# A new hand-written order for every instruction of a Fourier filter and a gated MLP that share one core

## The chip, the cores and the metric

The kernel runs on one core of a Trainium2 chip. The metric is device time in microseconds (us) of one execution. Three runs of the kernel before took 201.26, 201.38 and 201.50 us, median 201.38. The profiled execution took 201.59 us, of which 199.8 us lie between its first and its last instruction; that stretch is called the span, and times "at 125.7 us" count from its start.

## The reference, cut to what matters

```python
def _A_ref(x, w_r, w_i):                       # x: 1 x 2048 x 640
    X = jnp.fft.rfft2(x.astype(jnp.float32), axes=(-2, -1))
    X = X * (w_r + 1j * w_i)                   # weights: 2048 x 321
    return jnp.fft.irfft2(X, s=(S, D), axes=(-2, -1)).astype(jnp.bfloat16)

def _B_ref(x, w_gate, w_up, w_down):           # 640 x 1536, 640 x 1536, 1536 x 640
    g = jnp.einsum("bsd,df->bsf", x, w_gate)
    u = jnp.einsum("bsd,df->bsf", x, w_up)
    return jnp.einsum("bsf,fd->bsd", g * u, w_down)

xn = _layernorm(A_x)                           # over the 640 columns
return A_x + _A_ref(xn, A_w_r, A_w_i) + _B_ref(xn, B_w_gate, B_w_up, B_w_down)
```

Inputs and output are bfloat16. Both branches take the same normalized rows, and their results are summed with the input.

## The kernel before, in words

**Tasks.** `_build` makes a list of 971 tasks. A task is one copy, one transfer, or a short group of instructions for one engine, and has a number, a name, and the tasks that it depends on. The names used below:

- `T0_b` transposes a normalized block of 128 rows on TensorE, and `eT0_b` copies the result from PSUM to SBUF. There are 16 blocks b.
- `GU_f_r_u` (L945) is one gate or up product (u is 0 or 1) for a slice f of 128 hidden columns and four blocks of rows from r: five matmuls with 512 columns. `eG_f_r_u` copies it out of PSUM, and `H_f_r` (L985) multiplies gate by up on VectorE.
- The Fourier branch: `S1` to `S5` on VectorE and `R_b` (L899) with its copy `eR_b` are the forward transform's first stage. `D_t_w` (L1028) with its copies `eD_t_w_g`, then `C_t` (L1047), finish it. `WM_t` (L1064, L1067; five VectorE instructions that read PSUM) multiplies by the filter weights, and `SM_t` (L1080, L1081) combines the parts. `JA`, `JB`, `JC` and `JD` are four copies that mirror the result, the last two on GpSimd. `IA_q` (L1110) with the copy `eIA_q`, `I_a` (L1138) with the copy `eI_a`, and `V1` to `V5` on VectorE go back.
- `ACC_a_h_k` (L1215) is a part of the down projection for row block a and half h: k is the first of its hidden slices, counted in the order 7 to 11, 0 to 6. `IV_a_h` (L1227) adds the Fourier branch's last step in the same PSUM bank. `FINA_a_h` on ScalarE copies the sum out, `FIN_a` (L1254) on VectorE adds the input block that `ld_xr a` fetched, and `st_out a` writes it. Two output buffers are used in turn, so `FINA_5_0` waits until the store of block 3 has landed.

**Order.** Nothing is scheduled at run time. `_PLAN` is a literal table of 971 triples (task number, engine, PSUM bank), with engine 0 = TensorE (PE), 1 = ScalarE (ACT), 2 = VectorE (DVE), 3 = GpSimd (POOL), 4 = SyncE (SP), and bank -1 where the task takes none. `replay` reads it from top to bottom: each engine's instructions stand in the order in which their triples stand. It also adds the dependences that follow from the banks: a task that takes a bank waits for the copies that empty that bank's last owner. `compute_waits` turns the dependences into semaphore waits. So a triple that moves changes an engine's order, a changed second number moves a copy to another engine, and a changed third number makes a matmul wait for other copies. The cost functions (`_d_act` and the others) are not used at run time.

**Engines.** Copies out of PSUM and two of the mirror copies may stand on ACT or on DVE; L682 is the ACT form, L683 the other. SP issues 131 of the 133 transfers, strictly in its list's order: a transfer that waits for a buffer holds up all that stand behind it.

**Shared memory.** The down-projection weights lie in buffer `WD`. The tables for `IA` lie in the same place, in its first part, so `ld_wd0` waits for `IA_0` to `IA_9`, `ld_wd2` for `IA_10` to `IA_19`, `ld_wd4` for `IA_20` to `IA_29` and `ld_wd6` for `IA_30` and `IA_31`. Only `ld_wd7` (slices 7 to 11) is free of them. The first `ACC_a_h_5` needs `ld_wd0` and `ld_wd2`; the first `ACC_a_h_9` needs `ld_wd4` and `ld_wd6`. The filter weights of two steps t share one of three buffers, so `ld_w14_*` waits for `WM_8` and `WM_9`, and `WM_15` and `WM_14` wait for all `ld_w14_*`.

Of the kernel before, what the change touches and what calls it, by code (L numbers as in the profile page):

```python
# [400 lines left out]
def _d_act(n):  # L401
# [4 lines left out]
    (10, 0, 0), (11, 4, -1), (18, 2, -1), (12, 1, -1), (19, 2, -1), (20, 2, -1), (0, 3, -1), (8, 3, -1), (13, 4, -1),  # L406
    (182, 1, -1), (14, 4, -1), (15, 4, -1), (181, 4, -1), (21, 1, -1), (22, 2, -1), (23, 2, -1), (24, 0, 2), (9, 0, 7),
    (25, 2, -1), (26, 2, -1), (193, 0, 6), (27, 1, -1), (28, 1, -1), (29, 1, -1), (30, 2, -1), (31, 2, -1), (32, 0, 0),
    (43, 1, -1), (44, 1, -1), (183, 4, -1), (36, 2, -1), (34, 2, -1), (33, 2, -1), (35, 2, -1), (45, 1, -1), (46, 2, -1),
    (37, 2, -1), (47, 2, -1), (191, 0, 3), (192, 1, -1), (194, 1, -1), (38, 1, -1), (39, 2, -1), (195, 2, -1), (40, 2, -1),  # L410
    (124, 2, -1), (203, 0, 4), (196, 0, 2), (48, 0, 5), (197, 1, -1), (204, 1, -1), (49, 1, -1), (201, 0, 0), (202, 1, -1),
    (41, 0, 2), (42, 1, -1), (205, 2, -1), (184, 4, -1), (16, 4, -1), (53, 2, -1), (125, 2, -1), (54, 2, -1), (198, 0, 3),
    (199, 1, -1), (200, 2, -1), (64, 1, -1), (55, 2, -1), (50, 2, -1), (51, 2, -1), (208, 0, 1), (209, 1, -1), (206, 0, 7),
    (207, 1, -1), (65, 1, -1), (218, 0, 2), (219, 1, -1), (66, 1, -1), (67, 1, -1), (216, 0, 4), (217, 1, -1), (68, 1, -1),
    (210, 2, -1), (126, 2, -1), (52, 2, -1), (127, 2, -1), (56, 1, -1), (57, 2, -1), (69, 2, -1), (58, 2, -1), (73, 2, -1),
    (70, 2, -1), (128, 2, -1), (211, 0, 3), (212, 1, -1), (213, 0, 0), (214, 1, -1), (215, 2, -1), (186, 4, -1), (223, 0, 5),
    (185, 4, -1), (221, 0, 7), (224, 1, -1), (17, 4, -1), (76, 1, -1), (74, 0, 5), (71, 0, 6), (1, 4, -1), (129, 0, 3),
    (131, 0, 1), (222, 1, -1), (75, 2, -1), (220, 2, -1), (133, 2, -1), (61, 2, -1), (225, 2, -1), (134, 2, -1), (59, 0, 7),
    (72, 1, -1), (77, 1, -1), (132, 1, -1), (130, 1, -1), (78, 1, -1), (60, 2, -1), (135, 2, -1), (226, 0, 5), (227, 1, -1),
    (79, 1, -1), (80, 1, -1), (81, 2, -1), (228, 0, 0), (229, 1, -1), (230, 2, -1), (187, 4, -1), (62, 0, 6), (63, 1, -1),  # L420
    (231, 0, 1), (232, 1, -1), (136, 2, -1), (188, 4, -1), (7, 4, -1), (82, 2, -1), (233, 0, 3), (234, 1, -1), (88, 1, -1),
    (235, 2, -1), (137, 2, -1), (142, 2, -1), (238, 0, 4), (239, 1, -1), (236, 0, 0), (5, 4, -1), (190, 4, -1), (189, 4, -1),
    (241, 0, 1), (237, 1, -1), (89, 1, -1), (240, 2, -1), (85, 2, -1), (138, 0, 2), (139, 1, -1), (243, 0, 5), (244, 1, -1),
    (90, 1, -1), (242, 1, -1), (245, 2, -1), (143, 2, -1), (246, 0, 0), (247, 1, -1), (91, 1, -1), (140, 0, 2), (248, 0, 4),
    (249, 1, -1), (250, 2, -1), (144, 2, -1), (100, 1, -1), (251, 0, 6), (252, 1, -1), (253, 0, 0), (256, 0, 7), (481, 4, -1),
    (258, 0, 4), (92, 1, -1), (101, 1, -1), (141, 1, -1), (254, 1, -1), (257, 1, -1), (102, 1, -1), (255, 2, -1), (145, 2, -1),
    (93, 2, -1), (259, 1, -1), (260, 2, -1), (146, 2, -1), (261, 0, 5), (97, 2, -1), (263, 0, 1), (262, 1, -1), (449, 4, -1),
    (452, 4, -1), (3, 4, -1), (448, 4, -1), (450, 4, -1), (264, 1, -1), (103, 1, -1), (104, 1, -1), (105, 2, -1), (268, 0, 0),
    (269, 1, -1), (265, 2, -1), (106, 2, -1), (94, 2, -1), (155, 2, -1), (273, 0, 3), (151, 0, 4), (274, 1, -1), (152, 1, -1),
    (149, 0, 1), (150, 1, -1), (266, 0, 0), (267, 1, -1), (112, 1, -1), (270, 2, -1), (156, 2, -1), (153, 0, 5), (147, 0, 3),  # L430
    (154, 1, -1), (278, 0, 7), (279, 1, -1), (95, 0, 1), (96, 1, -1), (113, 1, -1), (271, 0, 2), (272, 1, -1), (275, 2, -1),
    (109, 2, -1), (276, 0, 6), (277, 1, -1), (280, 2, -1), (157, 2, -1), (485, 4, -1), (148, 1, -1), (281, 0, 0), (86, 0, 7),
    (114, 1, -1), (282, 1, -1), (283, 0, 2), (284, 1, -1), (115, 1, -1), (116, 1, -1), (285, 2, -1), (117, 2, -1), (158, 2, -1),
    (118, 2, -1), (159, 2, -1), (121, 2, -1), (453, 4, -1), (441, 4, -1), (482, 4, -1), (695, 4, -1), (444, 4, -1), (446, 4, -1),
    (443, 4, -1), (480, 4, -1), (442, 4, -1), (447, 4, -1), (478, 4, -1), (445, 4, -1), (2, 4, -1), (83, 0, 1), (110, 0, 6),
    (98, 0, 5), (291, 0, 3), (292, 1, -1), (84, 1, -1), (87, 1, -1), (111, 1, -1), (288, 0, 0), (289, 1, -1), (286, 0, 2),
    (287, 1, -1), (290, 2, -1), (99, 1, -1), (296, 0, 3), (297, 1, -1), (293, 0, 1), (294, 1, -1), (168, 2, -1), (295, 2, -1),
    (119, 0, 0), (120, 1, -1), (122, 0, 2), (162, 0, 3), (163, 1, -1), (298, 0, 7), (299, 1, -1), (164, 0, 0), (165, 1, -1),
    (166, 0, 5), (167, 1, -1), (303, 0, 4), (107, 0, 0), (300, 2, -1), (169, 2, -1), (451, 4, -1), (454, 4, -1), (304, 1, -1),
    (108, 1, -1), (301, 0, 3), (302, 1, -1), (160, 0, 4), (305, 2, -1), (170, 2, -1), (123, 1, -1), (308, 0, 6), (309, 1, -1),  # L440
    (161, 1, -1), (306, 0, 3), (307, 1, -1), (310, 2, -1), (316, 0, 2), (317, 1, -1), (313, 0, 1), (314, 1, -1), (171, 2, -1),
    (172, 2, -1), (323, 0, 5), (324, 1, -1), (321, 0, 7), (173, 0, 5), (179, 0, 0), (180, 1, -1), (175, 0, 3), (176, 1, -1),
    (322, 2, -1), (311, 0, 2), (174, 2, -1), (177, 0, 0), (509, 4, -1), (513, 4, -1), (4, 4, -1), (484, 4, -1), (312, 2, -1),
    (325, 2, -1), (315, 2, -1), (318, 0, 7), (319, 2, -1), (320, 2, -1), (178, 1, -1), (455, 0, 5), (457, 1, -1), (458, 0, 3),
    (460, 1, -1), (459, 1, -1), (456, 2, -1), (489, 0, 1), (346, 0, 0), (491, 2, -1), (490, 1, -1), (328, 0, 7), (329, 1, -1),
    (347, 1, -1), (461, 0, 4), (462, 2, -1), (333, 0, 3), (334, 1, -1), (463, 0, 6), (486, 0, 1), (487, 1, -1), (488, 1, -1),
    (331, 0, 0), (332, 1, -1), (464, 2, -1), (479, 4, -1), (483, 4, -1), (512, 4, -1), (510, 4, -1), (541, 4, -1), (514, 4, -1),
    (465, 2, -1), (468, 3, -1), (469, 3, -1), (466, 2, -1), (520, 0, 3), (511, 4, -1), (545, 4, -1), (543, 4, -1), (516, 4, -1),
    (522, 1, -1), (521, 1, -1), (326, 0, 5), (327, 1, -1), (330, 2, -1), (467, 2, -1), (335, 2, -1), (336, 0, 7), (337, 1, -1),
    (517, 0, 1), (338, 0, 0), (519, 1, -1), (339, 1, -1), (492, 0, 3), (518, 1, -1), (493, 2, -1), (494, 0, 6), (495, 2, -1),  # L450
    (341, 0, 5), (342, 1, -1), (358, 0, 0), (474, 0, 5), (475, 1, -1), (359, 1, -1), (551, 0, 2), (553, 1, -1), (552, 2, -1),
    (361, 0, 1), (362, 1, -1), (476, 0, 4), (477, 1, -1), (343, 0, 5), (472, 0, 6), (344, 1, -1), (548, 0, 1), (550, 1, -1),
    (470, 0, 3), (549, 1, -1), (471, 1, -1), (353, 0, 0), (496, 2, -1), (473, 2, -1), (542, 4, -1), (515, 4, -1), (523, 0, 5),
    (354, 1, -1), (348, 0, 7), (349, 1, -1), (497, 2, -1), (499, 3, -1), (500, 3, -1), (498, 2, -1), (503, 0, 3), (504, 1, -1),
    (540, 4, -1), (572, 4, -1), (573, 4, -1), (544, 4, -1), (546, 4, -1), (547, 4, -1), (524, 2, -1), (525, 0, 1), (526, 2, -1),
    (340, 2, -1), (574, 4, -1), (527, 2, -1), (345, 2, -1), (576, 4, -1), (608, 4, -1), (607, 4, -1), (605, 4, -1), (501, 0, 0),
    (530, 3, -1), (531, 3, -1), (571, 4, -1), (578, 4, -1), (577, 4, -1), (575, 4, -1), (502, 1, -1), (528, 2, -1), (529, 2, -1),
    (350, 2, -1), (371, 0, 4), (372, 1, -1), (505, 0, 0), (506, 1, -1), (582, 0, 6), (583, 1, -1), (356, 0, 5), (357, 1, -1),
    (507, 0, 4), (579, 0, 2), (581, 1, -1), (584, 1, -1), (508, 1, -1), (378, 0, 1), (368, 0, 5), (580, 1, -1), (556, 0, 6),
# [879 lines left out]
```

## Time and profile before

| what | value |
|---|---|
| median of three runs | 201.38 us |
| profiled execution, whole | 201.59 us |
| its span | 199.8 us |
| PE busy, instructions | 194.2 us (97%), x1612 |
| DVE busy, instructions | 180.6 us (90%), x376 |
| ACT busy, instructions | 138.2 us (69%), x280 |
| POOL busy, instructions | 12.8 us (6%), x22 |
| HBM read, written | 18.89 MB, 2.62 MB |
| granted TensorE clock | 1.000 |

The work falls into three stretches that overlap: loads, layer norm and first transposes (to about 17 us), GU products beside the Fourier branch (to about 135 us), and the down projection with the additions and stores (to the end). In the stretches of 10 us between 10 and 130 us, PE is busy for 9.8 us or more in each, and DVE for 9.0 us or more. ACT is busy for 9.8 us or more in each from 10 to 60 us, then for 6.5 to 9.3 us until 130 us, and for 1.3 to 5.1 us per stretch between 140 and 190 us.

Busy time of PE counts matmuls from their start to their modelled end. The steps between successive groups of matmuls say how fast it goes: five matmuls of a GU take 1.08 us when nothing holds them, which is 216 ns for each; three of an ACC take 0.41 us, 136 ns each.

### The profile page before, as it was taken

What the parts mean: (1) busy time and instruction counts of PE and PEld (TensorE: products, weight loads), DVE (VectorE), ACT (ScalarE), POOL (GpSimd) and SP (SyncE); (2) the same over time, 40 slices, a digit from 0 to 9 for tenths busy, and PEclk for the clock granted to TensorE, in tenths of its full rate; (3) what the DMA queues carried; (4) which work ended last, traced back from release to release, by engine and by line L of the source; (5) the groups of instructions that cost most, each with busy time, mean ns of one, the idle gap of its engine ahead of it and who ended that gap; (6) DMA issues with size and microseconds to landing.
All of it is one profiled execution on the core that took longest, in us unless ns stands there. A gap on an engine that the chain in (4) does not pass through costs nothing.

```text
span 199.8 us, 4175 instructions
## 1 busy us (share of the span) xinstructions
PE 194.2 (97%) x1612; PEld 124.3 (62%) x1629; DVE 180.6 (90%) x376; ACT 138.2 (69%) x280; POOL 12.8 (6%) x22
## 2 busy tenths in 40 slices
PE   8899999999999999999999999999999999999995
PEld 8897544455464555555555555557677767777774
DVE  2799999999999889999999999987999999998922
ACT  3899999999997689888898787576205551341230
POOL 1000000000000002122131120220000000000000
PEclk9999999999999999999999999999999999999999
DMA  6999602300079062343153640007002232036332
GB/s 180 330 367 329 215 0 68 79 3 0 0 228 289 13 168 62 91 119 79 38 154 98 152 135 0 0 3 228 7 0 88 73 105 92 16 102 187 98 102 66
DMA packets 21603, 21.78 MB, mean 109 GB/s; under 512 B 2384, under 2 KB 19536, under 8 KB 21456
## 3 DMA queue, kind: packets, MB, share of 16 engines
q1 hardware_dynamic: 20784, 21.11, 36.4%
q10 hardware_dynamic: 800, 0.41, 0.7%
q8 instruction: 13, 0.21, 0.5%
q14 instruction: 6, 0.05, 0.1%
HBM read 18.89 MB, written 2.62 MB: 108 GB/s over the span
## 4 chain that ended last, share of the span: by engine, by line
PE 53%; DVE 26%; ACT 12%; DMA 4%; issue 2%; SPq 2%; DVEq 0%
PE ps L945 23%; PE ps L1215 20%; DVE arena L1064 8%; ACT arena L682 7%; DVE arena L985 4%; DVE arena L683 3%; DVE arena L1081 2%; DVE arena L1080 2%; PE ps L715 2%; ACT arena L737 2%; DMA out_dram<-arena 2%; DVE arena L1067 2%; ACT arena L746 2%; DMA arena<-in_B_w_down_dram 2%; PE ps L899 2%
## 5 line engine op out<-in xcount | busy, mean ns | idle before, releaser
L682 ACT ACTIVATE arena<-ps 128x512 bf16<-128x512 f32 (+6 forms) x219 | 116.4, 590 | 52.4 <-PE ps L1227 19.6
L945 PE MATMUL ps<-arena 128*128 128x512 bf16 x423 | 100.0, 379 | 0.9
L945 PEld LDWEIGHTS ps<-arena 128*128 128x128 bf16 x440 | 40.8, 98 | 41.4
L1215 PE MATMUL ps<-arena 128*128 128x320 bf16 (+2 forms) x396 | 57.0, 295 | 0.8 <-DMA arena<-in_B_w_down_dram 0.4
L1215 PEld LDWEIGHTS ps<-arena 128*128 128x128 bf16 x396 | 37.6, 98 | 14.5 <-issue 0.7
L1064 DVE TENSOR_TENSOR arena<-ps,arena 128x256 bf16<-128x256 f32 x64 | 22.6, 415 | 0.8 <-PE ps L1047 0.7
L985 DVE TENSOR_TENSOR arena<-arena 128x512 bf16<-128x512 bf16 x44 | 18.6, 424 | 0.7 <-ACT arena L682 0.2
L683 DVE CAST arena<-ps 128x512 bf16<-128x512 f32 (+3 forms) x16 | 10.4, 658 | 1.8 <-PE ps L945 1.1
L1254 DVE TENSOR_TENSOR arena<-arena 128x640 bf16<-128x640 bf16 x15 | 7.0, 487 | 5.1 <-ACT arena L682 5.0
L1110 PEld LDWEIGHTS ps<-arena 128*128 128x128 bf16 x160 | 8.1, 117 | 4.0 <-DVE arena L1067 1.3
L746 ACT ACTIVATE arena<-arena 128x640 bf16<-128x640 bf16 x12 | 10.5, 877 | 0.1
L1094 POOL TENSOR_SCALAR arena<-arena 64x252 bf16<-64x252 bf16 x8 | 8.5, 1059 | 30.1 <-DVE arena L1081 29.8
L967 PE MATMUL ps<-arena 128*128 128x128 bf16 (+1 forms) x120 | 9.7, 237 | 0.5 <-DVE arena L683 0.5
L683 POOL COPY arena<-arena 64x252 bf16<-64x252 bf16 x8 | 3.8, 480 | 89.4 <-DVE arena L1081 89.1
L737 ACT ACTIVATE arena<-arena 128x640 bf16<-128x640 bf16 x12 | 9.3, 778 | 0.1
L967 PEld LDWEIGHTS ps<-arena 128*128 128x128 bf16 x120 | 8.4, 98 | 1.3 <-issue 0.6
L1110 PE MATMUL ps<-arena 128*128 128x64 bf16 x160 | 8.8, 198 | 0.0
L1227 PE MATMUL ps<-arena 128*128 128x320 bf16 (+2 forms) x33 | 8.3, 295 | 0.0
L851 DVE TENSOR_TENSOR arena<-arena 128x768 f32<-128x768 bf16 (+1 forms) x10 | 7.9, 793 | 0.1
L1028 PE MATMUL ps<-arena 128*128 128x64 bf16 (+1 forms) x160 | 7.0, 193 | 0.0
L1028 PEld LDWEIGHTS ps<-arena 128*128 128x128 bf16 x160 | 6.2, 98 | 1.3 <-issue 0.2
L1067 DVE TENSOR_TENSOR arena<-ps,arena 128x260 bf16<-128x260 f32 x16 | 6.9, 432 | 0.0
(60 smaller groups left out, 196.0 us busy)
## 6 DMA issues: line engine op xcount, KB each, us to landing
arena<-in_A_x_dram SPq DMA_DIRECT2D x19, 160.0 KB, 3.2
arena<-in_A_w_r_dram SPq DMA_DIRECT2D x30, 80.2 KB, 2.2
arena<-in_A_w_i_dram SPq DMA_DIRECT2D x30, 80.2 KB, 2.2
out_dram<-arena SPq DMA_DIRECT2D x15, 160.0 KB, 1.8
arena<-in_B_w_gate_dram SPq DMA_DIRECT2D x4, 320.0 KB, 6.5
arena<-in_A_x_dram SPq DMA_DIRECT2D x1, 1280.0 KB, 9.6
arena<-c_tf SPq DMA_DIRECT2D x4, 256.0 KB, 4.0
arena<-c_ti SPq DMA_DIRECT2D x2, 512.0 KB, 6.1
```

Source lines behind the costliest of these rows:

```text
L682: return c.e.activation(dst, src, _ACTF.Copy)
L683: return c.e.tensor_copy(dst, src)
L737: return c.e.activation(v_jk, v_x[:, b, :], _ACTF.Copy, scale=1.0 / _D, accum_out=v_m32[:, b:b + 1])
L746: return c.e.activation(v_jk, v_x[:, b, :], _ACTF.Square, scale=-1.0, bias=v_m32[:, b:b + 1], accum_out=v_ss[:, b:b + 1])
L945: ins = c.e.matmul(ps[:, bk, :], v_gw[:, w, j, ft, :], v_xt[:, j, rows], start=(j == 0), stop=(j == 4))
L967: ins = c.e.matmul(ps[:, bk, i * n:(i + 1) * n], v_gw[:, w, j, ft0 + i, :], v_xt[:, j, rows], start=(j == 0), stop=(j == 4))
L985: return c.e.tensor_tensor(v_ht[:, ft0, rows], gb[:, 0, :], gb[:, 1, :], _OP.mult)
L1028: ins = c.e.matmul(ps[:, bk + i, k * 64:k * 64 + n], v_uq[:, k, t + i, :], v_fd[:, k * 128 + w * n: k * 128 + w * n + n], start=True, stop ...
L1064: c.e.tensor_tensor(dst, xh, wv, _OP.mult)
L1067: return c.e.tensor_tensor(d5, x5, wt[:, :, :, 0:321:5], _OP.mult)
L1110: ins = c.e.matmul(ps[:, bk, 64 * k:64 * k + 64], yl, v_ti[:, q, 0, :], start=True, stop=True)
L1215: ins = c.e.matmul(ps[:, bk, 0:sl3.stop - sl3.start], v_ht[:, ft, a * 128:(a + 1) * 128], v_wd[:, ft, sl3], start=(ft == _FT_ORDER[0]), st ...
```

## The change

Only `_PLAN` is replaced. The same 971 tasks appear, every one once, and every instruction's shape is unchanged. The orders of PE, ACT, DVE, POOL and SP change, so do most bank numbers, and 23 tasks change their engine:

- ACT to DVE: `eR_15`, `eG_1_8_0`, `eG_8_12_1`, `eG_9_12_1`, `eD_0_1_0`, `eIA_17`, `JB_11`, `eIA_24`, `eIA_27`, `JB_15`, `eIA_29`, `eI_3`
- DVE to ACT: `eG_0_8_0`, `eG_11_8_0`, `eG_5_12_0`, `eG_6_12_0`, `eG_11_12_1`, `eD_2_1_1`, `eD_6_1_0`, `JA_9`, `eIA_18`, `eIA_30`, `eI_0`

The whole diff is 108 lines of triples against 108. The rows that the prediction leans on, with the numbers of the tasks: 406 `GU_5_12_0` and 407 its copy, 594 `IA_16`, 670 `ld_w14_1_2`, 695 to 699 `ld_wd7`, `ld_wd0`, `ld_wd2`, `ld_wd4`, `ld_wd6`; 757, 770, 783, 796 `ld_xr0`, `ld_xr1`, `ld_xr2`, `ld_xr3`.

```diff
-    (118, 2, -1), (159, 2, -1), (121, 2, -1), (453, 4, -1), (441, 4, -1), (482, 4, -1), (695, 4, -1), (444, 4, -1), (446, 4, -1),
...
-    (650, 2, -1), (405, 2, -1), (651, 2, -1), (655, 3, -1), (654, 3, -1), (406, 0, 2), (652, 2, -1), (407, 2, -1), (653, 2, -1),
...
-    (665, 4, -1), (680, 0, 2), (681, 2, -1), (697, 4, -1), (437, 1, -1), (408, 0, 1), (660, 0, 7), (409, 1, -1), (696, 4, -1),
...
-    (698, 4, -1), (691, 0, 4), (783, 4, -1), (757, 4, -1), (796, 4, -1), (690, 1, -1), (694, 1, -1), (421, 0, 0), (688, 2, -1),
...
+    (416, 0, 2), (417, 1, -1), (675, 0, 0), (676, 1, -1), (695, 4, -1), (620, 2, -1), (385, 2, -1), (621, 2, -1), (622, 2, -1),
+    (677, 1, -1), (639, 4, -1), (401, 0, 6), (633, 4, -1), (638, 4, -1), (601, 1, -1), (696, 4, -1), (667, 4, -1), (665, 4, -1),
...
+    (668, 4, -1), (623, 3, -1), (624, 3, -1), (650, 2, -1), (395, 2, -1), (398, 0, 2), (594, 0, 0), (697, 4, -1), (595, 1, -1),
...
+    (652, 2, -1), (424, 2, -1), (625, 0, 2), (631, 0, 3), (632, 1, -1), (627, 0, 5), (670, 4, -1), (406, 0, 0), (407, 1, -1),
...
+    (698, 4, -1), (785, 0, -1), (790, 0, -1), (771, 0, 5), (760, 0, -1), (791, 0, -1), (763, 0, 0), (764, 0, -1), (710, 2, -1),
```

What it does at the places named later, as each engine's list has it:

| place | before | after |
|---|---|---|
| SP, around the down-projection weights | `wd7` at place 28; after all `w14`: `wd2 wd0 wd4 xr2 xr0 xr3 wd6 xr1` | `wd7` at 79, `wd0` at 83; then the `w14` pieces with `wd2` ahead of the last, `w14_1_2`; then `xr2 wd6 xr0 wd4 xr3 xr1` |
| PE, between the last `IA` and the first `ACC_a_h_9` | 12 tasks: `GU_8_12_0`, `I` seven times, four parts of ACC | 19 tasks: `GU_9_12_1`, `GU_8_12_0`, `I` eight times, nine parts of ACC |
| the two banks of `C_15` | one was that of `GU_5_12_0`, copied on DVE behind `JA_13` | those of `IA_20` and `GU_10_12_0`; `GU_5_12_0` is copied on ACT |
| ACT, out of the first ACC banks | `eI_13, FINA_5_0, FINA_4_0, eI_12, FINA_5_1, FINA_4_1` | `eI_13, FINA_4_0, FINA_4_1, FINA_5_0, eI_12, FINA_5_1` |
| the bank of `ACC_5_1_0` | that of `ACC_5_0` | that of `ACC_4_0` |
| ACT, at the start | `sd_2` behind `eG_0_0_1` | `sd_2` ahead of `eG_0_0_0` |
| DVE, ahead of `SM_15` | `eG_0_8_0`, `eD_2_1_1`, `eD_6_1_0`, `eG_11_8_0`, `JA_9`, `eIA_18`, `eG_5_12_0`, `H_4_12` | instead of these: `eR_15`, `eD_0_1_0`, `eG_1_8_0`, `eIA_17`, `JB_11`, `eG_8_12_1` |

## The prediction

> **What bounds the kernel now.** I read the page's busy shares first, then the table of stretches, then the chain that ended last, and then the timeline at each place where TensorE (PE) pauses. Busy shares, and three stretches (columns: length, then busy time and instructions of PE, its weight loads, DVE, ACT, POOL, the clock, the DMA share, GB/s):
>
> ```profile
> PE 194.2 (97%) x1612; PEld 124.3 (62%) x1629; DVE 180.6 (90%) x376; ACT 138.2 (69%) x280; POOL 12.8 (6%) x22
> ```
>
> ```profile
> 30.00:40.00 10.00, 9.95 (x51) 4.70 (x51) 10.00 (x19) 10.00 (x24) 0.00 (x0) 1.00 0.30 74
> ...
> 120.00:130.00 10.00, 9.79 (x80) 5.26 (x80) 9.69 (x25) 6.45 (x15) 1.62 (x2) 1.00 0.00 0
> ...
> 160.00:170.00 10.00, 9.69 (x78) 7.01 (x77) 9.68 (x16) 3.14 (x7) 0.00 (x0) 1.00 0.30 96
> ```
>
> PE is nearly full everywhere, at full clock, with DVE close behind it. The Trainium skill (Perfetto Trace Analysis, "Identifying the Most-Contended Engine") calls matmul busy time a bad metric and points at weight-load busy time, here 62%. By that rule, up to 38% of the span might be recoverable. The trace's steps decide against it: in the chain, five 512-column matmuls take 1.08 us and twelve of the down projection 1.63 us, again and again. Walking along the weight loads task by task, and subtracting these steps, leaves few pauses between 9 us and the end. Three are above 0.3 us, 1.7 us together. The reordering can win about that much and little more; by the rule it could have been tens of us. The three, from the timeline:
>
> ```profile
> 124.94 0.68 DVE L683 CAST arena<-ps 128x512 bf16<-128x512 f32 x1
> ...
> 125.65 0.42 DVE L1094 TENSOR_SCALAR arena<-arena 64x1024 bf16<-64x1024 bf16 x1
> ```
>
> ```profile
> 125.76 0.43 PE L1047 MATMUL ps<-arena 128*128 128x321 bf16 x2 [0.16 <-DVE arena L683]
> ```
>
> `C_15` waits for one of its banks until DVE has copied `eG_5_12_0` out, which ends at 125.62. The five matmuls ahead of it have a step of 1.58 us instead of 1.08: **0.50 us**.
>
> ```profile
> 135.78 0.44 SPq L676
> ...
> 136.26 3.95 DMA arena<-in_B_w_down_dram
> ...
> 140.35 0.57 PE ps L1215 x3
> ```
>
> (From the chain: start, length.) `ld_wd6` is issued only at 136.26, behind three `ld_xr` on SP, lands 3.95 us later, and `ACC_3_1_9` starts then. The task before it has a step of 1.31 us instead of 0.68: **0.63 us**.
>
> ```profile
> 163.20 1.36 ACT L682 ACTIVATE arena<-ps 128x320 bf16<-128x320 f32 x3 [0.44 <-DMA out_dram<-arena]
> ...
> 163.69 1.34 PEld L1215 LDWEIGHTS ps<-arena 128*128 128x128 bf16 x11 [0.48 <-ACT arena L682]
> ```
>
> `ACC_5_1_0` takes the bank that `FINA_5_0` empties, and that waits for a store issued at 158.96 that took 4.22 us. `I_12` ahead of it has a step of 0.88 us instead of 0.28: **0.60 us**.
>
> **Part 1, the bank of `C_15`: -0.50 us.** After the change its banks were those of `IA_20` and `GU_10_12_0`. I follow ACT from the 112 us mark with this trace's rows: 613 ns for a 512-column copy, about 0.50 us from one start to the next in a row of them, 0.44 us for `eIA`, 0.70 us for `eD`. `eG_10_12_0` then ends at about 122.7, and `C_15`'s place is at about 123.9. The rule that speaks against giving ACT this copy is the Trainium skill's budget (ScalarE: Activation LUTs, "Rules for kernel authors"): 0.3 us plus 0.83 ns per element, an estimate of 0.72 us for 512. Five such copies between 119 and 124 us would then end about 1 us later, at 123.7, still in time. So both prices give the 0.50 us; I use the row. The chains of hand-over that get tight are `eG_3_12_1`, now behind `eIA_16` on ACT, ahead of `IA_20` (slack about 0), `eG_0_12_1` ahead of `IA_17` (0.1), and `WM_11` ahead of `GU_0_12_0` (0.4).
>
> **Part 2, the late weights: -0.63 us.** On SP `ld_wd6` now has one `ld_xr` ahead of it and `ld_wd4` two. Each issue takes 0.43 to 0.47 us, so after the last `IA` (about 132.6) they are issued by 134.1. With 3.95 us to landing, the longest of the four in this trace, they are there at 138.0. The Trainium skill (DMA: Bandwidth & Descriptors, "Anatomy of one DMA") has 2.0 us plus bytes/436e9, an estimate of 2.4 us for 160 KB. Taken for the kernel before, that would put `ld_wd6` at 138.7, ahead of its use, with no pause to win; the row says 140.21, so I go by the row. The work between the last `IA` and the first `ACC_a_h_9` was 1.08 + 7 x 0.28 + (3 x 0.68 + 0.54) = 5.6 us. Now it is 2 x 1.08 + 8 x 0.28 + (5 x 0.68 + 4 x 0.54) = 10.0 us. Need at 142.5, landing at 138.0: over 4 us in reserve.
>
> **Part 3, the bank of `ACC_5_1_0`: -0.60 us.** It now follows `FINA_4_0`, which stands ahead of `FINA_5_0` on ACT and needs the store of block 2. That is issued after `FIN_2` (about 155) and lands within 2.4 us; the bank is needed at 163. If the store takes 4.22 us, nothing changes.
>
> **Part 4, SP's other moves: 0.** `ld_ti1` and `ld_wd7` go far back: `ld_ti1` behind two `w10` pieces (about 93 us), `ld_wd7` to about 102. They took 7.9 and 6.8 us to land, so they are in by 101 and 109, and are used at 112 and 136. `ld_wd2` stands ahead of `ld_w14_1_2` and waits for `IA_16`, now at about 117.9. So that piece is issued at 118.7 and lands at 121 to 123 (w-loads took 2.0 to 4.5 us once the start was over). `WM_15` wants it at about 124.8. In the start, `gw8` now goes ahead of the second `gw6`. Adding the bytes at the landing rate of before (640 KB in 1.7 to 1.9 us, 320 KB in 1.1) puts `gw6_1` at 24.1, used at 24.9.
>
> **Part 5, the start: +0.15 us.** `sd_2` stands ahead of `eG_0_0_0` on ACT and waits for DVE until 9.2. That shifts ACT's next copies, and `eT0_2` comes to end at 12.4 instead of 12.07. `GU_0_2_1` needs it at 12.48 plus the 0.16 us that PE takes to see a copy end. Between nothing and 0.3 us; I take 0.15.
>
> **Part 6, DVE ahead of the last `IA`: +0.35 us.** Without the pauses PE comes to `IA_28` earlier; does DVE? Ahead of `SM_15`, 5.1 us of tasks leave DVE (three 512-column copies at 0.69, two `eD` at 0.82, `JA` 0.45, `eIA` 0.49, `H` 0.42), and 4.0 us come (0.81, 0.82, two at 0.69, 0.49, 0.48). `SM_15` ended at 131.37. It now ends 1.1 us earlier, and the 0.17 us wait of `WM_15` goes too: about 130.1. GpSimd's two copies took 1.62 us after that and PE 0.2 more: `IA_28` can start at about 131.95. PE's own place for it is 132.16 in the old time, less 0.50, less some 0.2 of smaller gaps between 95 and 107 us, plus 0.15: 131.6. So 0.35 us comes back as a new wait, with ends of 0 and 0.9.
>
> **Part 7, the rest.** The V chain on DVE decides when `IV` can run. It began at 137.94 because `V1_0` waited 0.70 us for `eI_3` on ACT; `eI_3` now stands on DVE, and I get 136.7. So the `V5` steps come 1.2 us earlier plus up to 0.7 from moved tasks, and `IV_4_1` and `IV_8_0`, which had 1.0 and 0.6 us to spare, keep it. `eI_14` now comes ahead of `V3_12` and makes DVE wait about 0.7 us for `I_14`, in front of `V5_12`, with over 1 us to spare. The smaller gaps (-0.2) and the tight hand-overs of part 1 and at 72 to 86 us (0 to 0.1 each, +0.2) cancel in my sum. The tail behind the last matmul (2.5 us) is the same.
>
> **Sum.** 201.59 - 0.50 - 0.63 - 0.60 + 0.15 + 0.35 = 200.36 us for an execution like the profiled one. That one lay 0.21 us above the median, so **200.1 us**.
>
> **Rivals.** *DVE holds the gain back* (24%): PE is ahead, but `SM_15` or the V chain comes hardly earlier. For it: DVE is busy 9.7 to 10.0 of 10 us from 80 to 130, and the chain runs along it there. Against it: the 1.1 us that leave. Then only the 0.6 us that `IV_8_0` had to spare remain: 200.8 us. *Nothing* (13%): the tight hand-overs on ACT cost 0.1 to 0.2 us at some ten places and eat the gain: 201.0 to 201.8 us. *ACT out of step* (13%, the slower side): between 105 and 120 us ACT gets `JA_9` (1.06 us) and copies whose matmul stands later on PE than the copy behind them. PE waits for ACT, ACT for PE's next task, and the lag isn't caught up, because DVE has no idle time there. It decides when ACT falls over 2 us behind PE, more than parts 1 to 3 bring; at 3 us it costs 202.4 us. ACT's idle time, 1.6 us in 110 to 120 and 3.5 in 120 to 130, speaks against it.
>
> **How the numbers follow.** The forecast's own range is 199.3 (all pauses gone, no new wait) to 200.7, with 50%. The 80% range adds most of the two next cases: 199.3 to 201.4. Differences below 0.2% (0.4 us) count as no change here. Faster: 50% + 24% = 74%; same 13%; slower 13%.
>
> **What would show it.** Right: no wait of `C_15` for DVE, of ACC for the down-projection weights, of ACC for `FINA` behind a store; `SM_15` ending near 130.1; `V1_0` starting near 136.7. Wrong: weight loads idle over 0.3 us with ACT as releaser between 100 and 125 us, `IA_28` behind GpSimd by over 1 us, or `WM_15` waiting for a w-load.

## The result and the profile after

The changed kernel takes 200.41 us (median of six runs, 200.26 to 200.47), the kernel before on the same chip 201.30 us (six runs, 200.82 to 201.50). The ratio is 0.996, with a 95% interval of 0.9946 to 0.9974: faster, by 0.9 us, and clear of the noise. The profiled execution took 200.44 us with a span of 198.7 us, at a clock of 0.999. Against 201.59 and 199.8 us that is 1.15 and 1.1 us less.

First the busy shares of the page of the changed kernel, and the same three stretches as before (length, then busy time and instructions of PE, its weight loads, DVE, ACT, POOL, the clock, the DMA share, GB/s):

```profile
PE 194.1 (98%) x1629; PEld 123.1 (62%) x1629; DVE 180.4 (91%) x377; ACT 137.8 (69%) x279; POOL 13.0 (7%) x22
```

```profile
30.00:40.00 10.00, 10.00 (x59) 5.03 (x58) 10.00 (x18) 9.94 (x24) 0.00 (x0) 1.00 0.48 122
120.00:130.00 10.00, 10.00 (x71) 5.07 (x68) 9.81 (x23) 6.04 (x13) 1.55 (x2) 1.00 0.07 24
160.00:170.00 10.00, 10.00 (x79) 7.27 (x78) 9.90 (x14) 3.38 (x8) 0.00 (x0) 1.00 0.33 88
```

The two late stretches, which held the pauses, have gone from 9.79 and 9.69 us of PE to 10.00. The shares of the whole page hardly moved. The chain that ended last tells more ("issue" is time in which an engine waited for nothing that the profile shows, SPq and the like are an engine's sequencer); here it is by engine, for the kernel before and then for the changed one:

```profile
PE 53%; DVE 26%; ACT 12%; DMA 4%; issue 2%; SPq 2%; DVEq 0%
```

```profile
PE 95%; DVE 1%; ACT 1%; DMA 1%; issue 0%; ACTq 0%
```

Before, the way back from the end leaves PE at every pause, through a copy or a transfer. Now it stays on PE nearly all the way. The waits of PE, the kernel before first and the changed one second (what waited for what: us in total, times, longest), name what went and what came:

```profile
PE ps L967 <- DVE arena L683: 0.5, 1, 0.5
PE ps L1215 <- DMA arena<-in_B_w_down_dram: 0.4, 1, 0.4
PE ps L1215 <- ACT arena L682: 0.3, 1, 0.3
PE ps L1047 <- DVE arena L683: 0.2, 1, 0.2
```

```profile
PE ps L808 <- DVE arena L796: 0.7, 2, 0.5
PE ps L967 <- DVE arena L683: 0.6, 1, 0.6
```

The last three rows of the first list are the three pauses of the prediction (the steps between weight loads gave 0.63, 0.60 and 0.50 us for them; this view counts from the modelled end of the matmul ahead, and leaves out waits below 0.15 us). None of the three is in the second list; what came to it belongs to the first 10 us, before PE can run freely.

To see where the time went, I walk along PE task by task, as the prediction did: the start of a task, less the full-speed steps of all tasks ahead of it. What is left is PE's loss up to there, in us. (Between kernels with one order on PE the differences are good to 0.02 us. Between the old order and the new one they are good to about 0.1: counted matmul by matmul instead of task by task, the last column is +0.09, -0.05, -0.64, -1.05.)

| up to | before | changed | difference |
|---|---|---|---|
| `GU_5_12_0` (119 us) | 5.04 | 5.20 | +0.16 |
| `GU_8_12_0`, behind the last `IA` (134 us) | 5.76 | 5.72 | -0.04 |
| `ACC_4_0_0` (151 us) | 6.52 | 5.87 | -0.65 |
| PE's last task (196 us) | 7.30 | 6.25 | -1.05 |

So the whole gain comes behind 134 us. Where the Fourier branch ends, the changed kernel is level with the old one, though `C_15` no longer waits. What took back the worth of that pause is one question for the experiments; whether the two later pauses need a new order of everything is the other.

### The profile page after: what moved, and what is told of

It is laid out like the page before. It is cut to its first block, busy times and chain, and to the rows that moved or that the text cites. A ratio compares the mean times of both kernels' runs of the same rounds, so it can differ in the third digit from the quotient of the medians.

```text
span 198.7 us, 4203 instructions
## 1 busy us (share of the span) xinstructions
PE 194.1 (98%) x1629; PEld 123.1 (62%) x1629; DVE 180.4 (91%) x377; ACT 137.8 (69%) x279; POOL 13.0 (7%) x22
## 4 chain that ended last, share of the span: by engine, by line
PE 95%; DVE 1%; ACT 1%; DMA 1%; issue 0%; ACTq 0%
PE ps L945 48%; PE ps L1215 26%; PE ps L967 4%; PE ps L1110 3%; PE ps L1028 2%; PE ps L1138 2%; PE ps L899 2%; PE ps L1047 2%; PE ps L808 2%; PE ps L1227 2%; DMA arena<-in_A_x_dram 1%; ACT arena L746 0%; DVE arena L755 0%; ACT arena L737 0%; DVE arena L683 0%
## 5 line engine op out<-in xcount | busy, mean ns | idle before, releaser
L945 PE MATMUL ps<-arena 128*128 128x512 bf16 x440 | 104.1, 379 | 0.0
L945 PEld LDWEIGHTS ps<-arena 128*128 128x128 bf16 x440 | 40.3, 98 | 40.8 <-DVE arena L1067 0.8
L1215 PEld LDWEIGHTS ps<-arena 128*128 128x128 bf16 x396 | 37.8, 98 | 13.5
L683 DVE CAST arena<-ps 128x320 bf16<-128x320 f32 (+3 forms) x16 | 9.7, 630 | 1.1 <-PE ps L899 0.6
L746 ACT ACTIVATE arena<-arena 128x640 bf16<-128x640 bf16 x12 | 10.2, 849 | 0.1
L1110 PEld LDWEIGHTS ps<-arena 128*128 128x128 bf16 x160 | 8.1, 116 | 3.2 <-ACT arena L682 0.3
L967 PEld LDWEIGHTS ps<-arena 128*128 128x128 bf16 x120 | 8.4, 98 | 1.4 <-issue 0.7
L737 ACT ACTIVATE arena<-arena 128x640 bf16<-128x640 bf16 x12 | 9.0, 751 | 0.2
L808 PE MATMUL ps<-arena 128*128 128x128 bf16 x80 | 6.8, 219 | 0.7 <-DVE arena L796 0.7
L1028 PEld LDWEIGHTS ps<-arena 128*128 128x128 bf16 x160 | 6.2, 98 | 1.8 <-issue 0.3
L808 PEld LDWEIGHTS ps<-arena 128*128 128x128 bf16 x80 | 5.3, 98 | 3.0 <-DVE arena L796 1.1
```

What stands on the lines that cost most here:

```text
L683: return c.e.tensor_copy(dst, src)
L746: return c.e.activation(v_jk, v_x[:, b, :], _ACTF.Square, scale=-1.0, bias=v_m32[:, b:b + 1], accum_out=v_ss[:, b:b + 1])
L808: ins = c.e.transpose(psb[:, bk * 1024 + o_: bk * 1024 + o_ + 128], v_x[:, b, j * 128:(j + 1) * 128], v_sm[:, 0, :])
L945: ins = c.e.matmul(ps[:, bk, :], v_gw[:, w, j, ft, :], v_xt[:, j, rows], start=(j == 0), stop=(j == 4))
L967: ins = c.e.matmul(ps[:, bk, i * n:(i + 1) * n], v_gw[:, w, j, ft0 + i, :], v_xt[:, j, rows], start=(j == 0), stop=(j == 4))
L1028: ins = c.e.matmul(ps[:, bk + i, k * 64:k * 64 + n], v_uq[:, k, t + i, :], v_fd[:, k * 128 + w * n: k * 128 + w * n + n], start=True, stop ...
```

## The experiments

Each was timed in five rounds against the kernel before, whose medians on these chips were 201.19 to 201.28 us. All times, and PE's loss at the same four places:

| kernel | median (runs from, to) | ratio, 95% interval | loss at `GU_5_12_0`, `GU_8_12_0`, `ACC_4_0_0`, end |
|---|---|---|---|
| before, loads | 201.21 (200.86, 201.68) | 0.9998 (0.9986, 1.0009) | 4.86, 5.59, 5.75, 6.79 |
| before, bank | 201.03 (200.54, 201.87) | 0.9991 (0.9974, 1.0007) | 5.02, 5.75, 6.99, 7.29 |
| before, loads and bank | 200.38 (200.35, 200.53) | 0.9960 (0.9946, 0.9974) | 4.98, 5.72, 5.88, 6.25 |
| before, copy | 200.94 (200.42, 201.97) | 0.9981 (0.9961, 1.0001) | 4.94, 5.34, 6.11, 6.42 |
| before, all three | 200.05 (199.99, 200.09) | 0.9940 (0.9924, 0.9955) | 4.92, 5.33, 5.49, 5.87 |
| changed, loads late | 200.41 (200.28, 200.50) | 0.9966 (0.9953, 0.9978) | 5.20, 5.73, 5.88, 6.27 |
| changed, copy | 200.14 (200.09, 200.18) | 0.9949 (0.9929, 0.9969) | 5.19, 5.47, 5.62, 6.00 |
| changed, banks, first | 200.68 (200.51, 200.80) | 0.9972 (0.9959, 0.9985) | 5.81, 6.08, 6.22, 6.61 |
| changed, copy and banks, first | 200.68 (200.60, 200.79) | 0.9974 (0.9962, 0.9986) | 5.81, 6.08, 6.22, 6.61 |
| changed, banks, second | 200.40 (200.30, 200.62) | 0.9956 (0.9940, 0.9971) | 5.11, 5.63, 5.78, 6.16 |
| changed, copy and banks, second | 200.11 (200.07, 200.14) | 0.9940 (0.9923, 0.9956) | 5.14, 5.40, 5.54, 5.93 |

### The three pauses one by one, in the old order

**Loads.** `ld_wd6` (699) goes from behind three `ld_xr` to behind `ld_wd4`.

```diff
-(698, 4, -1), (691, 0, 4), (783, 4, -1), (757, 4, -1), (796, 4, -1)
+(698, 4, -1), (691, 0, 4), (699, 4, -1), (783, 4, -1), (757, 4, -1), (796, 4, -1)
```

> The kernel before with one edit: SyncE issues the load wd6 right behind wd4, ahead of the three x row loads xr2, xr0 and xr3 that stood between them. Theory (the down projection's step stood 0.63 us for this load alone, and nothing is late right behind it): wd6 is issued about 1.3 us earlier, lands before 139.0, the long step at ACC_1_0_0 goes, and the kernel takes 0.6 us less than before, 200.7 us. Rival (the loss is only moved: the next wait, the bank of ACC_5_1_0 or DVE's chain V1 to V5, takes it up): 201.2 to 201.3 us, with the 0.60 us pause at 163 us grown or a new one between 140 and 165.

Measured: 201.21 us, no difference that can be told from none. `ld_wd6` landed at 137.50 instead of 140.21, and the pause was gone: between `GU_8_12_0` and `ACC_4_0_0` PE lost 0.16 us instead of 0.76. But the next pause grew from 0.60 to 0.86 us. The chain of this kernel, 157 to 165 us (start, length, what):

```profile
158.58 4.08 DMA out_dram<-arena
162.66 0.02 issue
162.68 0.45 ACT arena L682
163.13 0.05 issue
163.18 1.80 PE ps L1215 x12
```

The store of block 3 takes 4.08 us to land, `FINA_5_0` waits for it and `ACC_5_1_0` for `FINA_5_0`. PE came to `I_12` 0.77 us earlier than in the profile of before, the store landed only 0.52 us earlier (162.66 against 163.18), and 0.26 us of PE's gain were spent waiting. By the medians nearly all of the gain is gone: the rival, which named the bank of `ACC_5_1_0`, had the mechanism. That the runs without a profile lost the rest in the same way is likely, not shown.

**Bank.** `FINA_4_0` (814) goes ahead of `FINA_5_0` (827), and `ACC_5_1_0` (828) and `ACC_6_0_0` (836) exchange banks.

```diff
-(854, 0, 1), (827, 1, -1), (739, 0, 5), (814, 1, -1), (740, 1, -1), (828, 0, 2)
+(854, 0, 1), (814, 1, -1), (827, 1, -1), (739, 0, 5), (740, 1, -1), (828, 0, 0)
...
-(836, 0, 0)
+(836, 0, 2)
```

> The kernel before with one edit: FINA_4_0 goes ahead of FINA_5_0 on ACT, ACC_5_1_0 takes PSUM bank 0 (freed by FINA_4_0) and ACC_6_0_0 takes bank 2 (freed by FINA_5_0). Theory (ACC_5_1_0 waited only for the bank behind the store of block 3): the pause of 0.60 us at I_12 shrinks to 0.1 or less, ACC_6_0_0 doesn't wait, and the kernel takes 0.5 to 0.6 us less, 200.7 to 200.8 us. Rival (the next user of a late bank waits instead): 201.2 to 201.3 us.

Measured: 201.03 us; the interval takes in no change. The pause at `I_12` was gone in the profile, but in this execution the one ahead of it, for `ld_wd6`, was longer. The chain from 136.6 us:

```profile
136.67 4.01 DMA arena<-in_B_w_down_dram
140.69 0.14 issue
140.82 0.57 PE ps L1215 x3
```

`ld_wd6` was issued 0.41 us later than in the profile of before (136.67 against 136.26), because SP was held longer at an `ld_xr` (1.29 us instead of 0.86). PE lost 1.11 us instead of 0.63. So the old order's loss isn't a fixed sum: the landing of one load and of one store differs between these executions, and the runs of the kernel before and of these two lie 0.8 to 1.9 us apart.

**Loads and bank together.** Are the two waits one chain?

> The kernel before with the two edits of the down projection's stage together (wd6 behind wd4; FINA_4_0 ahead of FINA_5_0 with the two banks exchanged), without the copy moved to ACT. Alone they gave 0.07 and 0.25 us by the medians. Theory (the two waits stand one behind the other on PE, for transfers that land at their own time, so that PE time saved at the first is waited for at the second, and both must go): no wait for a transfer is left, 200.4 to 200.6 us, 0.45 us above the kernel with all three edits, and the runs lie within 0.2 us of each other instead of 1 us. Rival (the edits' gains add up as measured): 200.9 to 201.0 us, with a spread as before.

Measured: 200.38 us, all five runs within 0.18 us. Alone the edits gave 0.07 and 0.25 us by the medians (neither can be told from none), together 0.85. The theory holds: the two waits stand one behind the other, and PE waits at the second for a part of what it wins at the first, because the store does not land earlier by as much. And 200.38 is the changed kernel's 200.41: from `GU_8_12_0` to the end the two lose the same, to 0.01 us. Two moved triples and two changed banks give as much as the new order of all 971.

**Copy.** `eG_5_12_0` (407) goes to ACT, behind `eD_14_1_0` (676).

```diff
-(652, 2, -1), (407, 2, -1), (653, 2, -1)
+(652, 2, -1), (653, 2, -1)
...
-(676, 1, -1), (431, 0, 5)
+(676, 1, -1), (407, 1, -1), (431, 0, 5)
```

> The kernel before with one edit: the copy eG_5_12_0 goes from DVE to ACT, where it stands behind eD_14_1_0 in a gap of 1.07 us. Theory A (the pause is a true loss, and the changed kernel lost its worth again by other moves of the new order): C_15 starts 0.5 us earlier, WM_15, SM_15 and JC_15 end 0.5 to 0.7 us earlier, IA_28 starts at about 132.7 instead of 133.24, and the kernel takes 0.5 us less, 200.8 us. Rival B (in any order the chain SM_15, J, IA_28 or small PE waits between 126 and 133 us take the gain back): IA_28 at 133.1 or later, 201.2 to 201.3 us.

Measured: 200.94 us. `IA_28` started at 132.82 (theory A said about 132.7, rival B 133.1 or later). The loss at `GU_8_12_0` is 0.42 lower than before, but 0.10 of that was there at `GU_5_12_0`, ahead of the edit. (How much such a number varies by itself can be read off the first column: the kernel before and its five edits are alike up to 119 us, and have 4.86 to 5.04.) The edit's own part is 0.32 us, not 0.50. The weight loads of `C_15` and of the task behind it say why, first in the kernel before and then in this one, with the matmuls of this one's `C_15` below:

```profile
125.73 0.13 PEld L1047 LDWEIGHTS ps<-arena 128*128 128x128 bf16 x2 [0.62 <-issue]
125.90 0.88 PEld L945 LDWEIGHTS ps<-arena 128*128 128x128 bf16 x5
```

```profile
125.14 0.31 PEld L1047 LDWEIGHTS ps<-arena 128*128 128x128 bf16 x2
125.49 0.88 PEld L945 LDWEIGHTS ps<-arena 128*128 128x128 bf16 x5
```

```profile
125.36 0.44 PE L1047 MATMUL ps<-arena 128*128 128x321 bf16 x2
```

Without the wait, the first weight load of `C_15` starts 0.22 us ahead of its matmul (125.14 and 125.36), beside the last matmul of the task ahead. Behind the wait it starts 0.03 ahead (125.73 and 125.76, the row in the prediction). So a weight load that is 0.50 us late makes the matmul only 0.32 late. The step ahead of `C_15` fell from 1.58 to 1.08 us, but that of `C_15` itself grew from 0.17 to 0.35. The second and third pause, counted over two steps in the same way against the kernel with loads and bank, are worth 0.60 us (1.31 + 0.30 against 0.60 + 0.41) and 0.48 (0.88 + 0.56 against 0.36 + 0.60). That is 1.40 us for the three, not 1.73.

So theory A has the mechanism, with a smaller size. The median alone, with runs from 200.42 to 201.97, would not settle it. In this profile the second pause was still there (0.77 us from `GU_8_12_0` to `ACC_4_0_0`), and the third was not, as the store of block 3 landed after 2.55 us this time.

**All three.**

> The kernel before with the three single edits together: eG_5_12_0 on ACT, wd6 behind wd4, FINA_4_0 ahead of FINA_5_0 with the two banks exchanged; all other instructions in the old order. If the three pauses are independent and the rest of the new order brings nothing or costs: 1.6 to 1.7 us less than before, 199.6 to 199.7 us, so 0.7 us less than the changed kernel (200.41). If the first gain is taken back in any order: 1.1 to 1.2 us less, 200.1 to 200.2 us. If the pauses overlap and only the last one counts: 200.7 us.

Measured: 200.05 us, five runs within 0.10 us, 0.33 us below the kernel with two edits, as the two steps at `C_15` say (0.32). PE's loss at the end is 1.43 us lower than before, near the 1.40 of the three pauses; the median is 1.23 lower than that of the kernel before, and not 1.6. The time alone is nearest to the second case, the first gain taken back, but the trace rules that out: from `GU_5_12_0` to `GU_8_12_0` PE loses 0.41 us, against 0.74 with two edits. It is faster than the changed kernel, too: its slowest run (200.09) lies 0.17 us below the changed kernel's fastest (200.26). They ran in different sets, and the intervals of the two ratios overlap; the kernel before was 201.28 and 201.30 us in these sets. Its chain by engine:

```profile
PE 98%; DVE 1%; issue 0%
```

### What took the worth of the first pause back

From `GU_5_12_0` to `GU_8_12_0` the changed kernel lost 0.20 us less than the kernel before, of the 0.32 that the pause was worth, and it had lost 0.16 more ahead of that. In the new order `eG_5_12_0` went from DVE to ACT, and `eG_8_12_1` from ACT to DVE, to the same place: in front of `WM_15`. The timeline of the changed kernel, rows of DVE, POOL and PE's weight loads (start, length, engine, line, operation):

```profile
124.62 0.68 DVE L683 CAST arena<-ps 128x512 bf16<-128x512 f32 x1
125.33 1.42 DVE L1064 TENSOR_TENSOR arena<-ps,arena 128x256 bf16<-128x256 f32 x4
```

```profile
131.79 0.40 POOL L683 COPY arena<-arena 64x252 bf16<-64x252 bf16 x1
```

```profile
132.31 0.75 PEld L1110 LDWEIGHTS ps<-arena 128*128 128x128 bf16 x20 [0.35 <-ACT arena L682]
```

`C_15` was issued at 124.20, but `WM_15`, which needs it, only starts at 125.33, when the copy is out of the way. `WM_14`, `SM_15` and the mirror copies follow without a gap, `JC_15` on GpSimd ends at 132.19, and `IA_28` starts at 132.31. (The row names an ACT copy as the releaser. The ACT copy that ends ahead of it ended at 132.01, so the one that came last is GpSimd's.) From 111 to 134 us DVE's gaps of over 0.1 us add up to 0.1 us in the changed kernel, and to 0.9 before: at `IA_25` and `IA_28` DVE's chain paces PE.

**Copy, in the changed kernel.** `eG_8_12_1` (424) goes back to ACT.

```diff
-(652, 2, -1), (424, 2, -1)
+(652, 2, -1), (424, 1, -1)
```

> The changed kernel with one edit: the copy eG_8_12_1 goes from DVE, where it stands in front of WM_15, to ACT, into a gap of 0.89 us behind eG_3_12_1. Theory (DVE's chain WM_15, WM_14, SM_15, J holds two of PE's waits of 125 to 133 us: IA_25 for WM_14, 0.18, and IA_28 for JC_15, 0.23): SM_15 ends about 0.6 us earlier, at 129.9, JC_15 at 131.6, both waits go, and the kernel takes 0.3 to 0.45 us less than the changed one: 200.0 to 200.1 us. Rival (PE's own waits up to 125 us set IA_28): 200.3 to 200.5 us.

Measured: 200.14 us, 0.27 below the changed kernel, all runs below all of its runs, and below all of those of "changed, loads late", which was timed beside it and takes as long as the changed kernel. The same rows:

```profile
124.88 1.42 DVE L1064 TENSOR_TENSOR arena<-ps,arena 128x256 bf16<-128x256 f32 x4 [0.18 <-PE ps L1047]
```

```profile
131.31 0.40 POOL L683 COPY arena<-arena 64x252 bf16<-64x252 bf16 x1
```

```profile
131.88 0.92 PEld L1110 LDWEIGHTS ps<-arena 128*128 128x128 bf16 x20
```

Now DVE waits for PE at `WM_15`, `JC_15` ends at 131.71, and `IA_28` starts 0.43 us earlier with no wait. Two waits of PE went: `IA_25` for `WM_14`, and `IA_28`. The first is worth 0.18 us (a step of 0.53 against 0.35). The second is worth 0.05, as the weight load's lateness counts for less again (1.31 + 0.17 against 1.08 + 0.35); that is why the gain is below the 0.3 to 0.45 expected. So a quarter of a microsecond is shown to lie in this copy. From `GU_5_12_0` to `GU_8_12_0` this kernel loses 0.44 us less than the kernel before; what that is beyond the 0.32 of the pause (0.12, near the 0.1 to which the two orders can be compared) is not traced.

**Banks, first.** PE's weight loads in the changed kernel show small new waits, among them these two (in brackets the idle time ahead and its releaser):

```profile
110.96 0.76 PEld L945 LDWEIGHTS ps<-arena 128*128 128x128 bf16 x5 [0.41 <-DVE arena L1067]
...
122.07 0.76 PEld L945 LDWEIGHTS ps<-arena 128*128 128x128 bf16 x5 [0.35 <-DVE arena L1067]
```

They are `GU_0_12_0` and `GU_7_12_1`, each behind a `WM` that empties its bank. Other banks were to remove these two and a third, at 95 us: `GU_6_8_0` (351) and `GU_1_12_1` (388), `GU_0_12_0` (381), and `GU_9_12_0` (426) ahead of `GU_7_12_1`.

```diff
-(351, 0, 1), (352, 1, -1), (388, 0, 4)
+(351, 0, 4), (352, 1, -1), (388, 0, 1)
...
-(381, 0, 6)
+(381, 0, 1)
...
-(418, 0, 7), (419, 1, -1), (629, 0, 6), (426, 0, 4), (628, 1, -1), (427, 1, -1)
+(426, 0, 4), (418, 0, 7), (427, 1, -1), (419, 1, -1), (629, 0, 6), (628, 1, -1)
...
-(433, 0, 7)
+(433, 0, 0)
...
-(660, 0, 0)
+(660, 0, 7)
```

> The changed kernel with three of its small new waits of PE for a bank removed: GU_6_8_0 and GU_1_12_1 exchange banks 1 and 4 (worth 0.24 at 95 us), GU_0_12_0 takes bank 1 instead of 6 (0.24 at 111 us), GU_9_12_0 goes ahead of GU_7_12_1 with banks 0 and 7 exchanged behind it (0.23 at 122 us). DVE's work is untouched. Theory (WM_15 stands behind eG_8_12_1 on DVE, so that SM_15, JC_15 and with them IA_28 don't move): PE is up to 0.7 us earlier at 124 us and waits that much longer for WM_14 and JC_15; 200.3 to 200.5 us, no gain. Rival (the waits of PE add up): 199.7 to 199.8 us.

> The changed kernel with the edits of the two runs before it together (eG_8_12_1 on ACT, and the three exchanges of banks). Theory (PE's bank waits and DVE's chain are in parallel up to IA_28, and only with both shortened is the end earlier): IA_28 at about 131.6 instead of 132.3, 0.6 to 0.8 us less than the changed kernel, 199.6 to 199.8 us. If only DVE's chain counted: as with eG_8_12_1 alone, 200.0 us. If neither did: 200.4 us.

Measured: 200.68 us for both, 0.27 slower than the changed kernel. Both expectations missed, because `D_10_1` and `D_14_0` take banks 0 and 1 as a pair, and bank 1 now came free late. The weight loads of the first of the two, at 113 us:

```profile
113.11 0.35 PEld L1028 LDWEIGHTS ps<-arena 128*128 128x128 bf16 x10 [0.48 <-ACT arena L682]
```

That is `D_14_0`, behind `eG_0_12_0`, which ended at 113.06; `D_10_1` lost 0.37 us in the same way. A wait taken from one task was handed, larger, to the next owner of the bank. With such a delay on PE the copy on ACT was worth nothing either: at `WM_15` DVE stood idle for 0.52 us.

**Banks, second.** The same three waits, with banks that no pair asks for.

```diff
-(351, 0, 1)
+(351, 0, 4)
...
-(388, 0, 4)
+(388, 0, 5)
...
-(536, 0, 5)
+(536, 0, 4)
...
-(381, 0, 6)
+(381, 0, 2)
...
-(598, 0, 2)
+(598, 0, 6)
```

(538, 366 and 565 go to bank 5 and 393 and 386 to bank 4 along with them. The exchange around 122 us is that of the first try.)

> The changed kernel with the same three waits of PE for a bank removed in another way, since the first exchange put the wait on the next owner of the bank (D_10_1 and D_14_0 take banks 0 and 1 as a pair): GU_6_8_0, IA_10, GU_2_12_1 and GU_1_12_0 take bank 4, GU_1_12_1, IA_11, GU_9_8_0 and IA_13 bank 5, GU_0_12_0 and IA_18 exchange banks 6 and 2, and around 122 us GU_9_12_0 stays ahead of GU_7_12_1. DVE's order is untouched. Theory (DVE's chain WM_15, WM_14, SM_15, J sets IA_28): PE's loss at 124 us is 0.5 to 0.7 us smaller than in the changed kernel, JC_15 still ends at 132.0 to 132.2 and IA_28 starts at about 132.2; 200.3 to 200.4 us, a gain of 0.1 us or less. Rival (PE's waits add up): 199.7 to 199.9 us.

> The edits of the run before it, and eG_8_12_1 on ACT. Theory (two chains in parallel up to IA_28, both must be shortened): JC_15 ends at 131.4 to 131.6, IA_28 starts within 0.15 us of it, and the kernel takes 0.5 to 0.7 us less than the changed one, 199.7 to 199.9 us. Rival (only DVE's chain counts): 200.1 us, as with eG_8_12_1 alone.

Measured: 200.40 us without the copy, 200.11 with it. Without it the theory's main point held: `JC_15` ended at 132.10, `IA_28` started at 132.21, no gain in time. But PE's loss fell by 0.09 at `GU_5_12_0` and by 0.13 at `GU_10_12_1`, not by 0.5 to 0.7: most of what was saved at the three places was lost at other tasks ahead of 124 us, as at `IA_23`, which came right behind `WM_13` on DVE in both kernels (weight load at 119.53 and 119.44, 0.05 us behind its end). With the copy on ACT the banks bring 0.03 us beyond it, the number that the rival gave. That does not refute two chains in parallel, since PE's was hardly shortened. It is shown that in the changed kernel DVE's chain sets `IA_25` and `IA_28`. With the copy on ACT, PE waits at neither, and what a shorter way of PE up to 124 us would bring there is open.

**Loads late, in the changed kernel.** `ld_xr0` (757) and `ld_xr3` (796) go ahead of `ld_wd6` and `ld_wd4`.

```diff
-(699, 4, -1), (757, 4, -1)
+(757, 4, -1), (796, 4, -1), (699, 4, -1)
```

> The changed kernel with one edit: SyncE issues xr0 and xr3 ahead of wd6 and wd4 (xr2, xr0, xr3, wd6, wd4, xr1), much like the order of before. Theory (it is the new order of the down projection, which asks for these weights at 142.8 instead of 139.7, that removed the pause; the order on SyncE had 3.5 us to spare): wd4 lands 0.4 to 1.3 us later, at 139.7 to 140.6, ACC_0_0_9 starts without a wait, 200.3 to 200.5 us as the changed kernel. Rival (the order on SyncE removed it): a pause of 0.3 us or more at ACC_0_0_9, 200.7 us or above.

Measured: 200.41 us, as the changed kernel. `ld_wd4` landed at 139.60, and `ACC_0_0_9` started at 142.85 without a wait. So in the changed kernel the order on PE is enough to remove the pause: even a landing at 140.21, as before, would be in time. In the old order SP's alone did it too. Either is enough.

## Why the prediction was right, and where it was not

The sum for an execution like the profiled one was 200.36 us, and that execution took 200.44. The median was forecast at 200.1 and is 200.41, inside the range, and faster as expected. The mechanism was right: the three pauses went, and DVE took a part of the gain back ahead of the last `IA`. That the sum came within 0.08 us is partly luck, as the stages show, in PE's loss:

| stage | forecast | measured |
|---|---|---|
| up to `GU_5_12_0`: parts 5 and 7 | +0.15 | +0.16 |
| to `GU_8_12_0`: parts 1 and 6 | -0.50 + 0.35 = -0.15 | -0.20 |
| to `ACC_4_0_0`: part 2 | -0.63 | -0.61 |
| to the end: part 3 | -0.60 | -0.40 |

The three pauses were put at 1.73 us, by how late the weight loads were, and were worth 1.40. Against that, 0.1 us came outside of these stages, and the waits that came back in the second were put at 0.35 and cost 0.25 or less. (The differences between the two orders are good to 0.1 us only.)

**Part 1** had the mechanism, with a pause worth 0.32 us and not 0.50: `eG_10_12_0` ended at 122.86 (122.7), `C_15` came at 124.20 (123.9) and did not wait for DVE. The row was the better price, too: the copies on ACT took 0.60 us, 0.48 from start to start, not the estimate of 0.72 from the Trainium skill (ScalarE: Activation LUTs, "Rules for kernel authors"). The page gives its 0.3 us for an instruction whose bias is a pointer operand; these copies name no bias.

**Part 2** was right in its size, and in its reserve: need at 142.84 (142.5), landing at 139.32 (138.0). The landing was 1.3 us later than forecast, as SP was held 1.27 us at `ld_wd6` (0.43 to 0.47 was expected; what held it is not shown) and the last `IA` loaded its weights until 133.05, not 132.6. Still 3.5 us were left. (The 3.95 us to landing was not the longest of the four: `ld_wd0` took 4.09.)

**Part 3** removed the pause, which was worth 0.48 us and not 0.60, and 0.08 came back in the stage: `I_13` waits for `V5_4`, which ended at 159.37 (the step ahead of `I_13` is 0.86 us instead of 0.68, its own 0.25 instead of 0.36). `V1_0` began at 137.41 and not at 136.7, because PE came to `I_3` only at 135.79 and `eI_3` on DVE ended at 137.31. From there to `V5_4` DVE has no gap over 0.1 us, so the delay goes all the way. The prediction had named `IV_4_1` and `IV_8_0`, with 1.0 and 0.6 us to spare, and not `I_13`.

**Part 4** was right that these moves cost nothing: `w14_1_2` landed at 121.57 and `WM_15` wanted it at 125.33; `ti1` was in at 96.97, `wd7` at 110.64, the second `gw6` at 24.12 (24.1).

**Part 5** was wrong: `eT0_2` ended at 12.36 as foreseen (12.4), but `GU_0_2_1` started at 12.48 all the same, 0.12 us behind it. So the +0.16 of the first stage agrees with the +0.15 by luck. It came from elsewhere: at 27 us `GU_8_0_1` now waits for `H_5_0` on DVE, which reads the buffer that its copy will fill (`H_5_0` ended at 27.25, the weight load came at 27.37; before, 26.19 and 28.56), and PE loses about 0.15 us more there than before. The prediction did not see that wait.

**Part 6** had the mechanism. It forecast +0.35 for `IA_28` behind `SM_15` and the mirror copies; that wait made the weight load 0.23 us late and cost 0.05. `SM_15` ended at 130.49 (130.1). What it missed is that the same DVE chain held a second task: `IA_25`, for `WM_14`, at 0.18. It counted the copy that came to DVE in front of `WM_15` as one of several that move `SM_15` by their sum; that it stands where the removed one stood, and so gives back most of the worth of part 1, is shown by the run with `eG_8_12_1` on ACT, 0.27 us faster.

**The step that failed** is the last one, from the profiled execution to the median. I took 0.21 us off because the profiled execution of before lay so far above its median. But that excess fits the pauses, which stand for transfers whose landing differs from one execution to the next; with the pauses gone, it goes with them. The profiled execution of the changed kernel lies 0.03 us from its median, and its six runs lie within 0.21 us, against 0.68 for the kernel before. (One profile of each doesn't prove it: that of "before, loads and bank" lies 0.15 us above its median without such a wait.) So the gain by medians is 0.89 us, below the 1.15 us between the two profiles.

Of the rivals, "DVE holds the gain back" is true of part 1 alone, where DVE's chain ahead of `SM_15` took most of the gain. "ACT out of step" did not come: no weight load idles for more than 0.3 us behind ACT between 100 and 125 us. As to the Trainium skill's rule on weight-load busy time (Perfetto Trace Analysis, "Identifying the Most-Contended Engine"): in the kernel with all three edits it is 63%, while PE makes up 98% of the chain, so the 38% was not there to be won by a new order. The page names that measure together with MFU, the matmul work done as a share of the peak, which the prediction left out.

## What to carry to other kernels

Where a tuned kernel pauses in a few places, move only what each pause waits for before ordering everything anew: here two moved entries of the table and two changed banks gave as much as the new order, and one moved copy on top gave more than it. Fix pauses on one engine together, since one alone may only lengthen the next when that one waits for a transfer, and read a median that doesn't move against the trace. Count a pause over the step ahead of it and the task's own step, since a late weight load overstates it. When a copy leaves a full engine, look at what the new order puts into its place.

## What the hardware showed that I had not expected

- **One store lands later than the others, and after a time that varies.** `st_out3`, issued 1.0 us behind `ld_xr6` and 0.5 behind `ld_xr4`, landed after 4.22, 4.08, 4.83, 4.00, 2.55 and 4.01 us in the profiles of the kernel before and of its five edits, in the order of the table. The stores of the other blocks up to 14 took 1.8 to 2.6 us there, with the same bytes and the same queue; why this one takes longer is not shown. The estimate from the Trainium skill (DMA: Bandwidth & Descriptors, "Anatomy of one DMA"), 2.4 us for 160 KB, lies above the fastest (1.8) and below most of this one's; the page states it for transfers that GpSimd issues, and these are SyncE's.
- **The spread of the runs went with PE's waits for transfers.** The runs of the three edits that left one or both of the late waits differ by 0.82 to 1.55 us (12 runs each). The runs of the nine kernels whose profile has no wait of PE for a transfer behind 20 us differ by 0.07 to 0.32 us (5 to 12 runs each).
- **A weight load that comes late hides a part of its lateness.** At `C_15` it starts 0.22 us ahead of its matmul when nothing holds it, and 0.03 ahead when it had to wait: 0.50 us late on the weight load is 0.32 late on the matmul.
